# Running state by 64 tokens in place of 128, attention products on 64x64 quarters, every key turned by TensorE

## The chip, the cores and the metric

One Trainium2 chip; the kernel uses one of its cores. The metric is the device time of the launch in microseconds. Of the kernel before there are three timed runs and one profiled run.

## The reference

Decayed linear attention of four sequences of 768 tokens with eight heads of 64, and on its output a soft mixture of eight experts with four slots each. All data are float32.

```python
for b in range(nb):                                   # blocks of 64 tokens
    intra = np.einsum('bhic,bhjc->bhij', qb, kb) * Dmask[None]
    intra = np.einsum('bhij,bhjd->bhid', intra, vb)
    inter = np.einsum('bhid,bhde->bhie', qb * lam_pow[None], kv_state)
    out[:, :, sl] = intra + inter
    kv_state = lam_block * kv_state + np.einsum('bhsd,bhse->bhde', kb * rev_pow[None], vb)
...
logits = x @ phi                                      # x: 3072 x 512, phi: 512 x 32
d = softmax of logits over the tokens;  slot_input = d.T @ x
slot_out[e] = np.maximum(slot_input[e] @ w1[e], 0.0) @ w2[e]     # 8 experts, 512 -> 1024 -> 512
c = softmax of logits over the slots;   out = c @ slot_out
```

Dmask[i, j] is lam^(i-j) for i >= j and 0 above. The blocks are exact whatever their length, so a kernel may choose its own: it needs the masked product inside a block, the product of the decayed q with the state before the block, and the state's own step.

## The kernel before

The 3072 tokens are 24 chunks of 128 (T = 24, six to a sequence, NB = 6). The loop at line 442 takes one chunk a step. All engines run their instructions in the order in which the program writes them (the wrapper InOrder, whose line 51 all rows of the profile carry), so what stands in a step is set by that loop alone; nothing is reordered. A tile names a buffer; a pool gives a tile's tag so many buffers, and a writer waits until the readers of the buffer that it reuses are done.

A step does this. SP issues the loads of chunk t+2: q and k with the channels on the partitions, v with the tokens on them, and for nine of the chunks (loaded(), line 36) k a second time with the tokens on them, "kN". Between these it issues slabs of w1 (512 KB each), at a pace of PACE/10 a step up to NSLAB buffers; later loads of w2 ("w2t" of 256 KB into buffers that the attention leaves, "w2p" of 512 KB into slabs that the first expert product leaves) stand behind them. scores(t) multiplies k by q for pairs of 64 keys and 128 queries, on 64x64 quarters of the array, and DVE masks the two banks (at). recall(t) multiplies the state by the decayed q (qs, made by POOL) into the banks xa and xb. turn_k(t+1) transposes k on PE where it was not loaded, into the bank kv, and ACT copies it out (kn). natural(t-1) transposes a finished chunk (xt) back to tokens (x). attend(t) adds the masked products with v to xa and xb, 128 rows deep, and ACT copies them to xt. state(t) multiplies the decayed k (kd, POOL) by v into kv; DVE adds it to the decayed state (st), and POOL decays the sum for the next step (dec). Every fourth step has the logits of four chunks, the next one the transposes of their exponentials (weights), and the sums of the slots (slots) follow.

After the loop come the last chunk's part of the softmax, two first expert products (first, 64 matmuls each), two parts of the second (second), and the output, whose first tiles are written while the second part runs.

```python
442    for t in range(T):
463        scores(t)
467        recall(t)
471            turn_k(t + 1)
473                natural(t - 1)
488        attend(t)
501        decay_q(t + 1)
502        state(t)
503        decay_k(t + 1)
```

In the rows of the profile float32 matmuls have two records each, so that the 16 matmuls of scores are 32 records; transposes have one.

## Time and profile before

| | us |
|---|---|
| median of three runs | 169.73 (168.62 to 172.34) |
| the profiled execution | 170.31 |
| its span, from the first to the last instruction | 168.4 |
| PE busy in the span | 149.2 |
| DVE, POOL, ACT busy | 90.7, 64.4, 60.8 |
| DMA | 61.56 MB, mean 366 GB/s |

Times inside the profile count from the start of the span. "Busy" of PE is the union of its matmuls, weight loads are shown apart (PEld). The chain of waits follows the last instruction back to what released each piece of work. The page's groups give count, total busy time and the mean of one instruction in ns. Step 1 starts at 11.6 with its scores, step 22 at 106.3; the first expert product starts at 118.7.

### The profile page before, as it was taken

What the parts mean: (1) busy time and instruction counts of PE and PEld (TensorE: products, weight loads), DVE (VectorE), ACT (ScalarE), POOL (GpSimd) and SP (SyncE); (2) the same over time, 40 slices, a digit from 0 to 9 for tenths busy, and PEclk for the clock granted to TensorE, in tenths of its full rate; (3) what the DMA queues carried; (4) which work ended last, traced back from release to release, by engine and by line L of the source; (5) the groups of instructions that cost most, each with busy time, mean ns of one, the idle gap of its engine ahead of it and who ended that gap; (6) DMA issues with size and microseconds to landing.
All of it is one profiled execution on the core that took longest, in us unless ns stands there. A gap on an engine that the chain in (4) does not pass through costs nothing.

```text
span 168.4 us, 6282 instructions
## 1 busy us (share of the span) xinstructions
PE 149.2 (89%) x2629; PEld 108.0 (64%) x2629; DVE 90.7 (54%) x213; ACT 60.8 (36%) x153; POOL 64.4 (38%) x86
## 2 busy tenths in 40 slices
PE   6889998997979999979999799999899999999700
PEld 6668887686867889768868677776233345546600
DVE  2665453556475647565546537575118799245800
ACT  3033442443422444342344344225010698342700
POOL 1248772245665156655252556610000295000000
PEclk9999999999999999999999999999999999999965
DMA  5999999999999999999999999899999999999795
GB/s 170 350 330 308 373 399 409 410 407 407 416 405 405 374 402 404 408 415 405 407 409 386 387 329 337 261 289 273 390 399 408 411 399 408 403 375 314 262 384 195
DMA packets 32444, 61.56 MB, mean 366 GB/s; under 512 B 3616, under 2 KB 9760, under 8 KB 32416
## 3 DMA queue, kind: packets, MB, share of 16 engines
q1 hardware_dynamic: 32272, 61.16, 97.1%
q8 instruction: 21, 0.34, 0.8%
q14 instruction: 7, 0.06, 0.1%
q10 hardware_dynamic: 144, 0.01, 0.1%
HBM read 54.86 MB, written 6.29 MB: 363 GB/s over the span
## 4 chain that ended last, share of the span: by engine, by line
PE 65%; DMA 13%; DVE 10%; issue 4%; POOL 2%; ACT 1%; DVEq 0%; POOLq 0%; ACTq 0%; SPq 0%
PE xa L51 15%; PE kv L51 13%; PE sc L51 11%; PE gl L51 8%; PE xb L51 7%; PE tr L51 7%; PE dp L51 4%; DMA slab<-w_x 4%; DMA ld<-qT 4%; DMA ld<-kT 4%; DVE at L51 2%; DVE cs L51 2%; DVE CN L51 2%; DVE o L51 1%; DMA y<-o 1%
## 5 line engine op out<-in xcount | busy, mean ns | idle before, releaser
L51 DVE TENSOR_TENSOR at<-sc,mask 128x512 f32<-128x512 f32 x48 | 30.8, 683 | 9.9 <-PE sc L51 9.9
L51 PE MATMUL sc<-ld 64*64 64x128 f32 x768 | 27.8, 282 | 0.5 <-issue 0.5
L51 POOL TENSOR_TENSOR qs<-ld,qpow 128x512 f32<-128x512 f32 x20 | 25.7, 1285 | 5.9 <-DVE qpow L51 2.9
L51 PEld LDWEIGHTS sc<-ld 64*64 64x64 f32 x768 | 21.6, 136 | 6.4 <-issue 5.3
L51 ACT COPY x<-tr 128x512 f32<-128x512 f32 x24 | 14.1, 588 | 30.1 <-PE tr L51 30.1
L51 POOL TENSOR_TENSOR dec<-st,qpow 128x256 f32<-128x256 f32 x16 | 10.0, 622 | 28.1 <-DVE st L51 28.1
L51 PE MATMUL xa<-at,ld 128*64 128x128 f32 x192 | 15.8, 285 | 3.7 <-DVE at L51 3.7
L51 DVE TENSOR_TENSOR st<-dec,kv 128x256 f32<-128x256 f32 x16 | 6.8, 422 | 20.0 <-PE kv L51 20.0
L51 POOL TENSOR_TENSOR kd<-kn,mask 128x512 f32<-128x512 f32 x11 | 11.7, 1060 | 13.0 <-ACT kn L51 13.0
L51 PEld LDWEIGHTS xa<-at,ld 128*64 128x64 f32 x192 | 10.0, 136 | 8.3 <-DVE at L51 6.1
L51 ACT COPY kn<-kv 128x512 f32<-128x512 f32 x11 | 6.4, 586 | 23.9 <-PE kv L51 19.8
L51 PE MATMUL tr<-ident,xt 128*128 128x128 f32 x96 | 15.0, 279 | 0.0
L51 PE MATMUL xb<-at,ld 128*64 128x128 f32 x192 | 14.8, 275 | 0.0
L51 PE MATMUL kv<-ld,kd 128*64 128x64 f32 x320 | 12.8, 222 | 1.2 <-ACT kn L51 0.8
L51 PE MATMUL xa<-qs,st 64*64 64x128 f32 x160 | 12.3, 270 | 1.0 <-POOL dec L51 1.0
L51 PEld LDWEIGHTS kv<-ld,kd 128*64 128x64 f32 x320 | 12.1, 138 | 1.5 <-issue 1.5
L51 PE MATMUL xb<-qs,st 64*64 64x128 f32 x160 | 12.4, 270 | 0.0
L51 PEld LDWEIGHTS tr<-ident,xt 128*128 128x128 f32 x96 | 10.8, 142 | 2.4 <-issue 2.4
L51 POOL TENSOR_TENSOR kd<-ld,mask 128x512 f32<-128x512 f32 x9 | 9.5, 1060 | 5.1 <-DVE mask L51 5.0
L51 PEld LDWEIGHTS xb<-at,ld 128*64 128x64 f32 x192 | 10.8, 136 | 0.8 <-DVE at L51 0.7
L51 ACT COPY xt<-xa 128x256 f32<-128x256 f32 x24 | 8.8, 368 | 6.4 <-PE xa L51 6.3
L51 PEld LDWEIGHTS xa<-qs,st 64*64 64x64 f32 x160 | 9.5, 133 | 1.2 <-POOL dec L51 1.2
(134 smaller groups left out, 229.2 us busy)
## 6 DMA issues: line engine op xcount, KB each, us to landing
slab<-w_x SPq DMA_DIRECT2D x32, 512.0 KB, 6.9
w2p<-w_x SPq DMA_DIRECT2D x20, 512.0 KB, 9.4
ld<-qT SPq DMA_DIRECT2D x24, 256.0 KB, 6.2
ld<-kT SPq DMA_DIRECT2D x24, 256.0 KB, 5.8
ld<-vN SPq DMA_DIRECT2D x24, 256.0 KB, 6.9
w2t<-w_x SPq DMA_DIRECT2D x24, 256.0 KB, 5.4
y<-o SPq DMA_DIRECT2D x24, 256.0 KB, 3.5
ld<-kN SPq DMA_DIRECT2D x9, 256.0 KB, 5.6
```

The source lines that it names most:

```text
L51: return self._tc.keep_in_program_order(f(*args, **kwargs))
```

## The change

The state now goes forward by half a chunk, HF = 64 tokens. The masks and the powers are made for 64 positions, and every attention product works on a 64x64 quarter with 64 moving columns:

- scores: 16 matmuls as before, but each half of the keys meets its own half of the queries alone; DVE masks 256 columns a bank in place of 512.
- attend: each half of the tokens by itself. It comes in two calls. The first, "cross", takes for the rows of half j the heads of half 1-j; ACT reads two columns of its result (seen), and the second call, which does the other pairs, waits for that. gather() copies the finished banks to xt, as attend() did.
- recall: one product for each half of the chunk, with the state before that half. The first chunk of a sequence has one for its second half.
- state: 16 matmuls into two banks, ka and kb; DVE adds and decays twice (the decay was on POOL). The last chunk of a sequence, which had none, does the first half.
- k is turned on PE for all 24 chunks, two chunks ahead, with a bank of its own (tk); kN isn't loaded any more.
- scores(t+1) stand in step t, between the state's products and attend(t). Each step starts with state(t), and the logits run in one go with no step of the state between their parts.
- loads go as k four, v three and q four chunks ahead, ahead of the slabs; NLOAD 12 for 10, NSLAB 33 for 35, PACE 14 for 16.

TensorE's queue over a full step, before (here the step's scores are its last two rows, of 16 in all):

```order
L51 MATMUL kv<-ident,ld 128x128 x4
L51 MATMUL tr<-ident,xt 128x128 x4
L51 MATMUL xa<-at,ld 64x128 x4
L51 MATMUL xb<-at,ld 64x128 x4
L51 MATMUL kv<-ld,kd 64x64 x8
L51 MATMUL sc_726<-ld 64x128
L51 MATMUL sc_727<-ld 64x128
```

And TensorE's queue over the same work after the change, from the last rows of a step's scores to the first of the next step's state:

```order
L47 MATMUL sc_549<-ld 64x64
L47 MATMUL sc_550<-ld 64x64
L47 MATMUL xab<-at,ld 64x64 x8
L47 MATMUL tr<-ident,xt 128x128 x4
L47 MATMUL tk<-ident,ld 128x128 x4
L47 MATMUL xab<-at,ld 64x64 x8
L47 MATMUL xab<-qs,st 64x64 x16
L47 MATMUL ka<-ld,kd 64x64
L47 MATMUL kb<-ld,kd 64x64
```

The sizes are those of the result. The products of attend and of the state have twice the number at half the depth, the recall stands behind attend, and both transposes stand together between the two calls of attend.

DVE's queue over two steps without softmax work, before:

```order
L51 TENSOR_TENSOR at<-sc_726,mask 128x512
L51 TENSOR_TENSOR at<-sc_727,mask 128x512
L51 TENSOR_TENSOR st<-dec,kv 128x256
L51 TENSOR_TENSOR at<-sc_805,mask 128x512
L51 TENSOR_TENSOR at<-sc_806,mask 128x512
```

And after, one step and the start of the next:

```order
L47 TENSOR_TENSOR st<-dec,ka 128x256
L47 TENSOR_TENSOR dec<-st,qpow 128x256
L47 TENSOR_TENSOR at<-sc_1018,mask 128x256
L47 TENSOR_TENSOR at<-sc_1019,mask 128x256
L47 TENSOR_TENSOR st<-dec,kb 128x256
L47 TENSOR_TENSOR dec<-st,qpow 128x256
L47 TENSOR_TENSOR st<-dec,ka 128x256
```

Three instructions a step have become six, all of 256 columns, and the two decays came from POOL.

SP's queue from the last chunks' loads to the output, before:

```order
L51 DMA ld<-vN 128x512
L51 DMA ld<-kN 128x512
L51 DMA ld<-qT 128x512
L51 DMA ld<-kT 128x512
L51 DMA w2p<-w_x 128x2x512 x2
L51 DMA ld<-vN 128x512
L51 DMA w2t<-w_x 128x512 x24
L51 DMA w2p<-w_x 128x2x512 x17
L51 DMA y<-o 128x2x256 x24
```

And after:

```order
L47 DMA ld<-kT 128x512
L47 DMA ld<-vN 128x512
L47 DMA ld<-qT 128x512
L47 DMA slab<-w_x 128x1024 x2
L47 DMA ld<-vN 128x512
L47 DMA slab<-w_x 128x1024 x4
L47 DMA w2p<-w_x 128x2x512
L47 DMA w2t<-w_x 128x512 x24
L47 DMA w2p<-w_x 128x2x512 x19
L47 DMA y<-o 128x2x256 x24
```

Four slabs of w1 and a pair of w2 now stand behind the last load of the attention, where no slab stood, and 19 pairs behind the w2t in place of 17.

The diff, cut to what the steps below speak of (the line numbers of the kernel after are not those above):

```diff
+HF = P // 2
...
-NSLAB = 35
-NLOAD = 10
+NSLAB = 33
+NLOAD = 12
...
-PACE = 16
+PACE = 14
...
+    def load_step(s):
+        load("k", s + 2)
+        load("v", s + 1)
+        load("q", s + 2)
...
         for hp in range(HP):
             for j in range(2):
                 for hh in range(2):
                     r = slice(64 * hh, 64 * hh + 64)
+                    c = slice(hp * P + HF * j, hp * P + HF * j + HF)
                     pe.matmul(
-                        out=banks[hh][64 * j:64 * j + 64, hp * P:(hp + 1) * P],
-                        lhsT=k_[r, hp * P + 64 * j:hp * P + 64 * j + 64],
-                        rhs=q_[r, hp * P:(hp + 1) * P],
+                        out=banks[hh][HF * j:HF * j + HF, hp * HF:(hp + 1) * HF],
+                        lhsT=k_[r, c],
+                        rhs=q_[r, c],
                         start=True,
                         stop=True,
                     )
         AT[t] = []
         for hh in range(2):
-            at = work.tile([P, HP, P], F32, tag="at", name="at", bufs=2)
-            sc = banks[hh].rearrange("p (a b) -> p a b", a=HP)
+            at = work.tile([P, HP, HF], F32, tag="at", name="at", bufs=4)
+            sc = banks[hh][:, 0:HP * HF].rearrange("p (a b) -> p a b", a=HP)
             dve.tensor_tensor(out=at, in0=sc, in1=mask[:, hh], op=ALU.mult)
             AT[t].append(at)
     def decay_q(t):
...
+        if t >= T:
+            return
+        tk = bank("tk")
+        for hp in range(HP):
+            pe.transpose(tk[:, hp * P:(hp + 1) * P], IN["k", t][:, hp * P:(hp + 1) * P], ident)
+        KN[t] = tk
+    def keep_k(t):
+        if t >= T:
+            return
+        kn = work.tile([P, D], F32, tag="kn", name="kn")
+        act.copy(out=kn, in_=KN[t])
+        KN[t] = kn
+    def decay_k(t):
+        if t >= T:
+            return
+        kd = work.tile([P, H, DH], F32, tag="kd", name="kd")
+        pool.tensor_tensor(
+            out=kd.rearrange("p (a b) c -> p a b c", a=2),
+            in0=KN.pop(t).rearrange("p (b a c) -> p a b c", a=2, b=HP),
+            in1=kpow.rearrange("p (a b) o -> p a b o", a=2).broadcast_to([P, 2, HP, DH]),
+            op=ALU.mult,
+        )
...
+        KD[t] = kd
+    def state(t, j):
+        parts_ = 2 if t % NB < NB - 1 else 1
+        if j == 0:
+            v_ = IN["v", t].rearrange("p (h c) -> p h c", h=H)
+            kd = KD.pop(t)
+            KV[t] = [bank("ka"), bank("kb")][:parts_]
             for hp in range(HP):
+                for hh in range(2):
+                    for i, kv in enumerate(KV[t]):
+                        r = slice(HF * i, HF * i + HF)
+                        pe.matmul(
+                            out=kv[64 * hh:64 * hh + 64, hp * DH:(hp + 1) * DH],
+                            lhsT=kd[r, HP * hh + hp, :],
+                            rhs=v_[r, HP * hh + hp, :],
+                            start=True,
+                            stop=True,
+                        )
+            ST[t] = [ST["S"] if t % NB > 0 else None]
+        if j == parts_:
+            return
+        kvv = KV[t][j][:, 0:HP * DH].rearrange("p (a b) -> p a b", a=HP)
+        st = work.tile([P, HP, DH], F32, tag="st", name="st", bufs=4)
+        if t % NB == 0 and j == 0:
+            dve.tensor_copy(out=st, in_=kvv)
+        else:
+            dve.tensor_tensor(out=st, in0=ST["dec"], in1=kvv, op=ALU.add)
+        ST[t].append(st)
+        ST["S"] = st
+        if parts_ == 2:
+            dec = work.tile([P, HP, DH], F32, tag="dec", name="dec")
+            dve.tensor_tensor(out=dec, in0=st, in1=lamc.broadcast_to([P, HP, DH]), op=ALU.mult)
+            ST["dec"] = dec
...
         g, a = divmod(hp, 2)
+        return XB[t][hh][64 * a:64 * a + 64, g * P + HF * j:g * P + HF * j + HF]
+    def attend(t, cross):
+        if cross:
+            both = ps.tile([P, 2, 512], F32, tag="x", name="xab")
+            XB[t] = [both[:, hh] for hh in range(2)]
+        v_ = IN["v", t].rearrange("p (h c) -> p h c", h=H)
+        for hp in range(HP):
+            for j in range(2):
+                hh = 1 - j if cross else j
+                r = slice(HF * j, HF * j + HF)
+                pe.matmul(
+                    out=place(t, hh, hp, j),
+                    lhsT=v_[r, HP * hh + hp, :],
+                    rhs=AT[t][hh][r, hp, :],
+                    start=(cross and hp < 2),
+                    stop=True,
+                    skip_group_check=True,
+                )
+        if cross:
+            act.copy(out=seen, in_=both.rearrange("p a b -> p (a b)")[:, HF:513:512 - HF])
...
     def recall(t):
+        qs = QS.pop(t)
+        for j in range(2):
+            st = ST[t][j]
+            if st is None:
+                continue
             for hp in range(HP):
                 for hh in range(2):
                     r = slice(64 * hh, 64 * hh + 64)
                     pe.matmul(
+                        out=place(t, hh, hp, j),
                         lhsT=st[r, hp, :],
+                        rhs=qs[r, hp, j, :],
+                        start=False,
                         stop=True,
                         skip_group_check=True,
...
-        pl = bank("gl")
+        pl = bank("tk" if g == G - 1 else "sc0")
...
+    turn_k(0)
+    keep_k(0)
+    scores(0)
+    decay_k(0)
+    powers()
+    decay_q(0)
     for t in range(T):
...
+        last = t == T - 1
+        load_step(t + 2)
+        want = min(NSLAB, (t + 1) * PACE // 10 if t < T - 2 else NSLAB)
         load_early(want - sent)
         sent = max(sent, want)
...
-        for _ in range((2, 4, 3)[t - T + 3] if t >= T - 3 else 0):
+        for _ in range((8, 3)[t - T + 2] if t >= T - 2 else 0):
...
+        turn = t // 4 - 1 if t > 3 else None
+        if t == 0:
+            attend(0, True)
+            turn_k(1)
+            keep_k(1)
+        state(t, 0)
+        scores(t + 1)
+        state(t, 1)
+        decay_k(t + 1)
+        if t > 0:
+            attend(t, True)
+            natural(t - 1)
+        if last:
             load_one(work, "kd", 1)
             load_one(work, "kn", 1)
+            for _ in logits(G - 1):
+                pass
+        else:
+            turn_k(t + 2)
+            keep_k(t + 2)
+            if turn is not None and t % 4 == 0:
+                for _ in logits(turn):
+                    pass
+            if turn is not None and t % 4 == 1:
+                sm = slot_softmax(turn, weights())
+                next(sm)
+            if turn is not None and t % 4 == 2:
+                slots(turn)
+                for _ in sm:
+                    pass
+        attend(t, False)
+        recall(t)
+        gather(t)
+        if last:
+            break
+        decay_q(t + 1)
```

## The prediction

> **What bounds the kernel now.** I read the stages first, then the chain of waits, then the DMA part of the page. The first view gives the busy time of each engine in five stretches: the start, attention steps 1 to 21, the last two steps with the softmax that follows them, the expert products, and the writing out.

> ```profile
> core 0: us, PE busy (x) PEld busy (x) DVE busy (x) ACT busy (x) POOL busy (x), PEclk, DMA share, GB/s
> 0.00:11.60 11.60, 8.57 (x90) 7.37 (x90) 6.29 (x19) 2.82 (x5) 3.07 (x9) 1.00 0.82 293
> 11.60:106.30 94.70, 89.32 (x1920) 73.28 (x1920) 51.96 (x115) 34.62 (x92) 50.90 (x53) 1.00 1.02 389
> 106.30:118.70 12.40, 11.32 (x222) 8.78 (x220) 7.88 (x26) 4.31 (x13) 3.34 (x5) 1.00 0.89 269
> 118.70:151.50 32.80, 32.80 (x354) 13.30 (x354) 18.70 (x44) 14.65 (x35) 7.11 (x20) 1.00 1.05 400
> 151.50:168.40 16.90, 7.16 (x58) 5.32 (x58) 5.91 (x10) 4.37 (x9) 0.00 (x0) 0.78 0.83 289
> ```

> The second row is the stage that the change rewrites: 94.7 us for 21 steps. PE is busy for 89.3 us of it. The transfers move 389 GB/s, which is 94.7 x 0.389 = 36.8 MB; at the 400 GB/s of the fourth row that alone takes 92.1 us. So two resources are nearly full in this stage, and a gain on one is worth only the distance to the next.

> The chain of waits prices one whole step (start, us, what); the products between an earlier and a present state ("xa, xb" of a recall) fill 57.04 to 57.48.

> ```profile
> 55.54 0.46 PE kv L51 x16
> 56.00 1.03 PE sc L51 x32
> ...
> 57.48 0.59 PE kv L51 x4
> 58.06 0.44 PE tr L51 x4
> 58.50 0.59 PE xa L51 x8
> 59.09 0.44 PE xb L51 x8
> ...
> 61.58 1.01 PE gl L51 x32
> ...
> 65.55 0.37 PE dp L51 x2
> ...
> 67.85 0.99 PE gl L51 x8
> ```

> State 0.46, scores 1.03, recall 0.44, turning k 0.59, natural 0.44, attend 0.59 + 0.44: 3.99 us. The first piece after a change of tile shape is 0.15 dearer (0.59 against 0.44 for the same four transposes or eight matmuls), and that happens three times a step. Every four steps 1.01 + 0.37 + 0.99 come on top. For steps 1 to 21: 21 x 3.99, less 11 unturned k at 0.44, three missing states at 0.46 and three missing recalls at 0.44, plus five times 2.37, is 88.1 us, near the 89.3 of the row.

> **PE after the change.** What counts is how fast quarter products follow each other. The timeline of PE shows the recall, already on 64x64 quarters, with 128 moving columns.

> ```profile
> 56.86 0.27 PE L51 MATMUL xa<-qs,st 64*64 64x128 f32 x1
> 56.87 0.27 PE L51 MATMUL xb<-qs,st 64*64 64x128 f32 x1
> 56.87 0.27 PE L51 MATMUL xa<-qs,st 64*64 64x128 f32 x1
> 56.88 0.27 PE L51 MATMUL xb<-qs,st 64*64 64x128 f32 x1
> 56.97 0.27 PE L51 MATMUL xa<-qs,st 64*64 64x128 f32 x1
> ```

> Four start within 0.02 us and the next four 0.11 later: the quarters run side by side, and the columns set the pace. With 64 columns the state's row above has 16 records in eight pairs, 0.46 / 8 = 0.058 a pair. So I price a group of four with 64 columns at 0.058, 0.0145 a record. The lower bound is half of 0.11, 0.055; the upper is that the record rate seen here, 0.11 / 4 = 0.027, can't be beaten. I take 0.058, since the state's row has the same columns and the recall shows that four start nearly together.

> State, scores and recall become 32 records each, 8 x 0.058 = 0.47; attend splits into two times 16, 0.23 each; natural and turning stay at 0.44 each, and now every k is turned. Shapes change twice a step, not three times. Sum: 3 x 0.47 + 2 x 0.23 + 2 x 0.44 + 2 x 0.15 = 3.05. For 21 steps, less half a recall (0.23) in three, plus the same five times 2.37: 64.1 - 0.7 + 11.9 = 75.3, 12.8 less than 88.1.

> [...]

> **DVE and POOL.** The forms that change, from the page and the groups of instructions:

> ```profile
> L51 DVE TENSOR_TENSOR at<-sc,mask 128x512 f32<-128x512 f32 x48 | 30.8, 683 | 9.9 <-PE sc L51 9.9
> L51 POOL TENSOR_TENSOR dec<-st,qpow 128x256 f32<-128x256 f32 x16 | 10.0, 622 | 28.1 <-DVE st L51 28.1
> L51 DVE TENSOR_TENSOR st<-dec,kv 128x256 f32<-128x256 f32 x16 | 6.8, 422 | 20.0 <-PE kv L51 20.0
> L51 POOL TENSOR_TENSOR qs<-ld,qpow 128x512 f32<-128x512 f32 x20 | 25.7, 1285 | 5.9 <-DVE qpow L51 2.9 <-POOL kd L51 1.7 <-DMA ld<-qT 1.3
> L51 POOL TENSOR_TENSOR kd<-kn,mask 128x512 f32<-128x512 f32 x11 | 11.7, 1060 | 13.0 <-ACT kn L51 13.0
> ```

> In steps 1 to 21, 42 maskings shrink from 0.683 to 0.422 (the price of 256 columns in the state's row): -11.0. There are 39 state sums for 18: +8.9. 36 decays arrive from POOL, at 0.422 as well: +15.2. DVE goes from 52.0 to 65.1 before waits. POOL loses the decay and keeps 1.06 + 1.29 = 2.35 a step, under the 3.05 of PE.

> The new decay reads two tiles of SBUF. DVE's CN, of that form, shows what POOL does to it; the POOL rows are of the same moments.

> ```profile
> 38.25 0.89 DVE L51 TENSOR_TENSOR CN<-ce,cs 128x128 f32<-128x128 f32 x1
> ```
> ```profile
> 37.93 1.06 POOL L51 TENSOR_TENSOR kd<-kn,mask 128x512 f32<-128x512 f32 x1
> ```
> ```profile
> 57.19 0.29 DVE L51 TENSOR_TENSOR CN<-ce,cs 128x128 f32<-128x128 f32 x1
> ```
> ```profile
> 58.88 1.06 POOL L51 TENSOR_TENSOR kd<-kn,mask 128x512 f32<-128x512 f32 x1 [3.52 <-ACT kn L51]
> ```

> With POOL idle (3.52 us before 58.88) it takes 0.29; begun during a kd it takes 0.89 and ends just after it. So a decay costs between 0.42 and 0.42 + 1.29, a whole qs. Of the two in a step, the first falls on the qs that starts when the recall before has ended, some 0.4 left of it; the second falls behind the masks, when kd is about over. I take 0.4 for one in two, 18 x 0.4 = 7.2: DVE 72 us, below PE; all at 0.6 would make it 87. [...]

> **DMA.**

> ```profile
> HBM read 54.86 MB, written 6.29 MB: 363 GB/s over the span
> ...
> ld<-kN SPq DMA_DIRECT2D x9, 256.0 KB, 5.6
> ```

> A load of 256 KB is 0.262 MB. The nine natural k go: 2.36 MB, 5.9 us at 400 GB/s. Total traffic then needs (61.15 - 2.36) / 0.400 = 147 us. In steps 1 to 21 there are 63 loads and 29 slabs of 0.524 MB, 31.7 MB: 79 us. But PACE 14 and NSLAB 33 push weights behind step 21: then 2 slabs, 24 w2t, 20 w2p and the output remain, 1.05 + 6.29 + 10.49 + 6.29 = 24.1 MB. Before it was 12.4 x 0.269 + 32.8 x 0.400 + 16.9 x 0.289 = 21.3 MB in 62.1 us.

> **The sum.** Steps 1 to 21: DMA 79, PE 75.3, DVE 72. Before, the stage lay 2.6 above its highest bound (94.7 against 92.1). I add that, and 0.5 for each of five softmax steps: the logits now run in one go, their exponentials stand on ACT ahead of the copies out of xab, and the next step's first attend waits for those. Price, the ACT groups:

> ```profile
> L51 ACT ACTIVATE e<-gl,nm 128x128 f32<-128x128 f32 x5 | 1.8, 368 | 4.9 <-PE xa L51 4.9
> L51 ACT ACTIVATE alpha<-nm 128x1 f32<-128x1 f32 x5 | 1.4, 283 | 0.0
> ```

> 0.37 + 0.28 less what is free before the attend. That is 84.1; I round to 85 for three resources within 7 us of each other (bounds 79 and 94.7). The start stays at 11.6: a turning and two copies are added, half of the mask scans goes; bounds -1.5 and +1. After step 21, 24.1 MB at 400 GB/s is 60.3, plus what the last row loses by its 289 GB/s, 16.9 x (1 - 289/400) = 4.7: 65.0, if the hole in the third row (269 GB/s, 4.1 us) is filled by the two slabs, the w2p and the eight w2t that steps 20 to 22 now queue; 69 if not. PE's own tail is the old 62.1 and hides under it. Span 11.6 + 85 + 65 = 161.6. The profiled run took 170.31 for 168.4, 1.9 more: 163.5, against the median of 169.73 a gain of 3.7%. The new read of two columns ("seen") hides behind natural and turning, 0.88 us; uncovered it costs at most the 0.28 of alpha a step.

> **Rivals.**
> 1. DVE is the bound. For it: three kinds of its work grow, and the 0.89 of CN. At 0.6 on every decay plus 2.6 and 2.5 the stage takes 92, span 168.6, time 170.5; halfway 167. Against: idle POOL in the second half of a step. It decides from 0.5 on every decay.
> 2. Quarter records don't come faster than the 0.0275 that is the mean of the rows above. Place: the four quarter products, 128 records a step. A step costs 128 x 0.013 = 1.66 more, PE 75.3 + 35 = 110, stage 115, span 192, time 194: slower. It decides from about 0.019 a record: there 128 x 0.0045 x 21 = 12 us put PE at 87, and the stage, with 2.6 and 2.5, at 92, and the gain of 6.8 is gone. For it: no row shows a lower mean. Against: the spacing inside a group of four. [...]
> 3. The hole fills and the stage follows the DMA: the whole traffic 147 us, plus 2 at the start and 4.7 at the end: 154 to 157 with waits, time 156 to 159.
> A smaller one, more code to fetch, lies within the range:
> ```profile
> q8 instruction: 21, 0.34, 0.8%
> ```
> 1,200 more matmul records mean some nine packets more of 16 KB. What one costs PE no row shows; I take nothing, and the range's upper end has room for it.

> **Chances.** Forecast 0.52, its own range 159 to 168; rival 1 0.20; rival 2 0.15; rival 3 0.13. The range 156.5 to 173 leaves out most of rival 2 and a little of rival 1. About 2% is what a measurement tells from no change, 166.3 to 173.1. Faster: rival 3 and most of the forecast, 0.58. Same: the rest of it and most of rival 1, 0.23. Slower: rival 2 and the tail of rival 1, 0.19.

> **What would show it.** Right: scores of 32 records near 0.5 us, a step without softmax near 3.6 to 3.9, DVE's decay of 0.42 to 0.8, the stage to step 22 near 85, 0.40 TB/s from there to the last weights. Wrong: scores near 0.8 (rival 2); decays at 1 us and DVE back to back (rival 1); steps short but PE waiting for w2p in the second expert product, which would say that the weights were pushed too late and the 65 is the term that failed.

## The result, and the profile after

The changed kernel takes 200.47 us (median of four runs, 198.06 to 203.46), the kernel before 169.63 beside it: a ratio of 1.171, 95% interval 1.161 to 1.181. It is slower, by 31 us, where 6 us faster was forecast. Most kernels here have a slower state in some of their runs (202.59 and 203.46 beside 198.06 and 198.35 in this one), so differences are given between the lowest runs too: here 198.06 - 168.62 = 29 us. The profiled execution took 198.35 us with a span of 196.2.

The page of the changed kernel: the span, the busy times, PE's granted clock in tenths, the mean rate of the transfers, the queue of the instruction fetches, and the chain by engine.

```profile
span 196.2 us, 8808 instructions
...
PE 151.7 (77%) x3833; PEld 111.9 (57%) x3833; DVE 113.2 (58%) x278; ACT 71.4 (36%) x190; POOL 63.7 (32%) x78
...
PEclk9999995799987999999797999859999999999995
...
DMA packets 31157, 59.35 MB, mean 302 GB/s; under 512 B 3472, under 2 KB 9616, under 8 KB 31120
...
q8 instruction: 30, 0.49, 1.0%
...
PE 70%; issue 16%; DVE 9%; ACT 1%; DVEq 0%
```

No engine is full: PE fell from 89% of the span to 77, and the transfers from 366 to 302 GB/s. But "issue", time in which an engine waited for nothing that the profile shows, is 16% of the chain, where it was 4. The clock drops in several places.

The stages of the changed kernel (columns as in the prediction): attention steps 1 to 21 (step 22's first products start at 133.03, so the cut lies 1 us into it), and everything from the first expert product on.

```profile
11.60:134.00 122.40, 91.67 (x3024) 77.89 (x3025) 74.26 (x179) 44.30 (x126) 49.03 (x44) 0.90 0.83 287
```
```profile
146.30:196.20 49.90, 40.14 (x411) 18.66 (x411) 24.60 (x54) 19.05 (x43) 7.08 (x20) 0.95 1.01 362
```

From the first expert product it is 49.9 us, as before (118.7 to 168.4, 49.7). All of the loss lies ahead of that: 21 steps take 122 us, where 85 were forecast, and PE is busy in 92 of them.

What PE's time is made of shows in the chain of waits (start, us, what), at the largest "issue" rows:

```profile
22.00 2.53 issue
24.88 0.48 PE sc L47 x32
...
28.00 3.04 issue
...
53.32 3.21 issue
...
91.49 3.10 issue
...
124.01 2.64 issue
```

The products are quick: 0.48 for the 32 records of the scores. Between them PE stands still for up to 3.2 us. The timeline of PE shows where it stops, in the middle of a state's products, whose operands were there already:

```profile
27.73 0.23 PE L47 MATMUL kb<-ld,kd 64*64 64x64 f32 x2
27.78 0.22 PE L47 MATMUL ka<-ld,kd 64*64 64x64 f32 x1
31.04 0.26 PE L47 MATMUL kb<-ld,kd 64*64 64x64 f32 x1 [3.04 <-issue]
```

Next, the busy times in stretches that I cut at the ends of such stops. The counts in brackets behind PE and PEld are matmuls and weight loads:

```profile
18.80:24.53 5.73, 3.19 (x126) 2.87 (x127) 1.51 (x4) 1.88 (x5) 2.32 (x3) 1.00 0.98 335
24.53:31.03 6.50, 3.46 (x126) 3.00 (x126) 2.88 (x6) 1.88 (x5) 2.40 (x2) 0.95 0.93 337
...
50.00:56.50 6.50, 3.30 (x126) 2.80 (x126) 2.59 (x6) 1.98 (x5) 2.47 (x2) 1.00 0.91 332
56.50:61.00 4.50, 3.96 (x127) 3.57 (x127) 1.71 (x6) 1.29 (x5) 1.83 (x2) 0.63 0.57 194
```

Every stretch holds 252 to 254 records, whatever they are and however long it lasts; with PE's 105 semaphore and drain records, 3.5 a block on average, that is about 256. A packet of q8 is 16,384 bytes in the trace (0.49 MB / 30 on the page), which is 64 bytes for each of 256 instructions; and the 30 packets are one for every 256 of PE's 7,775 instructions (7,771 in the trace). So I read a stop as a wait for the next block of instructions. The DMA view around the stop of 28.00 agrees. From 24.6 to 28.6 us it has no packet of q8, from 28.6 to 29.7 it has this one, and from 29.7 to 31.0 none again:

```profile
q8 instruction: 1, 0.02, 5.8%
```

PE stops at 28.00; the packet comes 0.6 us later at the earliest, and PE goes on at 31.04, 1.3 us or more behind its end. So it is at every boundary: counted in steps of 256 rows of PE from 14.30 on, the first row behind each of the 24 boundaries up to 133 us starts 1.26 to 1.60 us after the end of a packet. The fetch is thus not hidden behind PE's work here: it sets the time of the stage.

### The profile page after: what moved, and what is told of

Its sections match the earlier page's. It is cut to its first block, busy times and chain, and to the rows that moved or that the text cites. A ratio compares the mean times of both kernels' runs of the same rounds, so it can differ in the third digit from the quotient of the medians.

```text
span 196.2 us, 8808 instructions
## 1 busy us (share of the span) xinstructions
PE 151.7 (77%) x3833; PEld 111.9 (57%) x3833; DVE 113.2 (58%) x278; ACT 71.4 (36%) x190; POOL 63.7 (32%) x78
## 3 DMA queue, kind: packets, MB, share of 16 engines
HBM read 52.50 MB, written 6.29 MB: 300 GB/s over the span
## 4 chain that ended last, share of the span: by engine, by line
PE 70%; issue 16%; DVE 9%; ACT 1%; DVEq 0%
PE xab L47 22%; PE sc L47 15%; PE ka L47 10%; PE tr L47 9%; PE tk L47 9%; PE kb L47 6%; DVE dec L47 2%; DVE at L47 2%; DVE st L47 1%; DVE o L47 1%; DVE acc L47 1%; DVE cs L47 1%; DVE CN L47 0%; DVE h L47 0%; ACT xt L47 0%
## 5 line engine op out<-in xcount | busy, mean ns | idle before, releaser
L47 POOL TENSOR_TENSOR qs<-ld,qpow 128x512 f32<-128x512 f32 (+1 forms) x24 | 28.4, 1182 | 66.4 <-issue 65.0
L47 PE MATMUL xab<-at,ld 64*64 64x64 f32 x768 | 25.0, 240 | 7.8 <-issue 6.6
L47 PEld LDWEIGHTS xab<-at,ld 64*64 64x64 f32 x768 | 18.5, 145 | 16.9 <-issue 14.5
L47 PE MATMUL sc<-ld 64*64 64x64 f32 x768 | 20.5, 236 | 8.6 <-issue 8.3
L47 DVE TENSOR_TENSOR dec<-st,qpow 128x256 f32<-128x256 f32 x40 | 24.9, 623 | 1.4
L47 PE MATMUL kb<-ld,kd 64*64 64x64 f32 x320 | 16.4, 241 | 7.9 <-issue 6.5
L47 PE MATMUL ka<-ld,kd 64*64 64x64 f32 x384 | 19.6, 236 | 3.7 <-issue 3.7
L47 DVE TENSOR_TENSOR at<-sc,mask 128x256 f32<-128x256 f32 x48 | 17.9, 414 | 7.2 <-PE sc L47 7.1
L47 PEld LDWEIGHTS ka<-ld,kd 64*64 64x64 f32 x384 | 16.4, 149 | 7.4 <-issue 7.4
L47 PE MATMUL xab<-qs,st 64*64 64x64 f32 x704 | 16.9, 231 | 0.2 <-issue 0.2
## 6 DMA issues: line engine op xcount, KB each, us to landing
ld<-kT SPq DMA_DIRECT2D x24, 256.0 KB, 5.6
ld<-qT SPq DMA_DIRECT2D x24, 256.0 KB, 4.2
ld<-vN SPq DMA_DIRECT2D x24, 256.0 KB, 4.5
w2t<-w_x SPq DMA_DIRECT2D x24, 256.0 KB, 5.0
y<-o SPq DMA_DIRECT2D x24, 256.0 KB, 3.4
```

What stands on the lines that cost most here:

```text
L47: return self._tc.keep_in_program_order(f(*args, **kwargs))
```

## The experiments

The theories: **F**, a block of 256 PE instructions takes some 5 us to come while the loads run, and the changed kernel's products use it up in less. **V**, the decay of the state on DVE, and its contention with POOL. **C**, the chain kn, kd, qs through ACT and POOL, with one buffer each.

**Fewer instructions, same columns.**

```diff
-        for j in range(2):
-            st = ST[t][j]
+        st = ST[t][0]
...
-                        rhs=qs[r, hp, j, :],
+                        rhs=qs[r, hp].rearrange("p j b -> p (j b)"),
```

> The changed kernel, but the recall multiplies all 128 queries of a chunk by the state at the chunk's start, in eight products of 128 columns in place of sixteen of 64. It leaves out the state at the middle of the chunk for the second 64 queries (that state is still made). TensorE's streamed columns are the same; about 160 products (some 640 to 770 of TensorE's 7,775 instructions, or three blocks of 256) are gone. Theory F (TensorE's instructions come in blocks of 256 and a block takes 5 to 6 us to arrive while the loads run): three blocks fewer, 12 to 18 us faster than the changed kernel, 182 to 189 us. Rivals V (VectorE with the decay of the state, or its shared access) and C (the chain of one-buffer tiles through ScalarE and GpSimd): nothing of theirs moves, 198 to 202 us.

Measured: 192.4 us (186.2 to 196.0), 8 us less than the changed kernel, 12 between the lowest runs (186.16 and 198.06), with 384 of PE's 3,833 matmul records gone. On F's side of the rivals' 198, and at the lower end of F's 12 to 18 or below it. The kernel leaves out a part of the recall, so its output is not the reference's.

**The kernel before, cut into small pieces.** This is the run that decides. Of the change it has the shorter products alone.

```diff
+            for i in range(2):
+                c = slice(hp * P + HF * i, hp * P + HF * i + HF)
...
-                        out=banks[hh][64 * j:64 * j + 64, hp * P:(hp + 1) * P],
-                        rhs=q_[r, hp * P:(hp + 1) * P],
+                            out=banks[hh][64 * j:64 * j + 64, c],
+                            rhs=q_[r, c],
...
-                        rhs=qs[r, hp, :],
+                        rhs=qs[r, hp, HF * i:HF * i + HF],
```

> The kernel before, complete, with each score product and each recall product of 128 columns issued as two of 64 columns: the same streamed columns, the same sums, the same work on every other engine, but 24 more products a chunk (TensorE's program grows from 5,358 to 7,534 instructions; the changed kernel has 7,775). At the changed kernel's rate for quarters of 64 columns (32 records in about 0.48 us) the 64 records of the scores take 0.96 us, where they took 1.03. Theory F: 8.5 blocks more at 5 to 6 us each against the 3.8 us a step of before, so it becomes about as slow as the changed kernel, 185 to 200 us, with stops of 1 to 3 us every 256 instructions. Rivals V and C, and any that lies in the changed kernel's decay, buffers or loads: no change, 168 to 172 us.

Measured: 199.3 us (194.5 to 201.1). With DVE, POOL, ACT, loads and buffers of the kernel before, it is about as slow as the changed kernel (200.5; between the lowest runs 194.5 against 198.1), so neither V nor C is needed to explain nearly all of the loss. Its page has 3,717 matmuls, and its stretches between two boundaries are again of 252 to 254 records:

```profile
PE 159.1 (83%) x3717; PEld 119.2 (62%) x3717; DVE 90.7 (47%) x213; ACT 61.2 (32%) x153; POOL 64.4 (33%) x86
```
```profile
28.27:33.80 5.53, 3.95 (x127) 3.50 (x126) 2.52 (x5) 1.33 (x3) 3.52 (x4) 1.00 0.93 313
33.80:38.54 4.74, 4.40 (x127) 3.76 (x127) 1.07 (x4) 1.59 (x5) 1.28 (x1) 1.00 0.97 322
```

The scores themselves are hardly slower in pieces: 64 records start within 0.98 us, against 0.92 for the 32 of the kernel before, and the recall's 32 within 0.63 against 0.55 for 16 (medians, first start to the next group's). That is 3 us in 24 steps, of the 30.

**The decay back on POOL.**

```diff
-            dve.tensor_tensor(out=dec, in0=st, in1=lamc.broadcast_to([P, HP, DH]), op=ALU.mult)
+            pool.tensor_tensor(out=dec, in0=st, in1=lamc.broadcast_to([P, HP, DH]), op=ALU.mult)
```

> The changed kernel, complete, with the decay of the state put back on GpSimd, where it was before; nothing else. Theory F: no change, 197 to 204 us. Rival V (VectorE's decay, 0.62 us on average, 40 times, and its contention with GpSimd hold up the chain): 5 to 15 us faster. Rival C (GpSimd's queue is the chain): 40 decays of about 1 us more on GpSimd, 5 to 20 us slower.

Measured: 202.5 us (195.2 to 206.5), no change that shows in this spread; the lowest run is 2.9 us below the changed kernel's lowest. V falls, which asked for 5 to 15 us less, and C as far as it lies in POOL's queue.

**Light loads**, in the changed kernel and later in the kernel before.

```diff
-        want = min(NSLAB, (t + 1) * PACE // 10 if t < T - 2 else NSLAB)
+        want = 0 if t < T - 2 else NSLAB
```

> The changed kernel, complete, with none of the 33 weight slabs loaded before step 22; all of them are asked for there. The whole is longer, since the transfers of the slabs now follow the attention (220 to 245 us); what counts is the time from 11.6 us to the end of step 21 and TensorE's stops in it, with only some 0.8 MB a step asked for. Theory F with a fetch that waits behind the loads: the stops go or shrink to under 0.5 us each and the stage goes from about 125 us to 85 to 95. Theory F with a fetch that is slow by itself: stops as before, stage 115 to 125. Rivals V and C: stage 115 to 125 with TensorE's waits on named tiles, not on nothing.

> The kernel before, complete, with none of its 35 weight slabs loaded before step 22, like the changed kernel with light loads, whose first expert product (the lookup of the last chunk's slots ahead of it) began 11.8 us earlier than with its own loads, at 134.0 in place of 145.9. What counts here is the same product, at 118.2 in the kernel before. If the loads hold up the kernel before through TensorE's fetch as they do the changed one, it comes 8 to 12 us earlier. If TensorE's columns set the stage and the fetch is just in time (a block resumes 1.25 to 2 us after its packet with a stop over 0.4 us only twice), it comes 0 to 5 us earlier, at 113 to 118, and stays 16 to 21 us ahead of the changed kernel with light loads: that part of the loss is then the fetch by itself, with no loads to wait behind.

Measured: 210.8 and 203.6 us in all. What counts is the stage. The busy times of 30 to 90 us, first of the changed kernel with its own loads, then with light ones, then of the kernel before with its own and with light loads:

```profile
30.00:90.00 60.00, 48.48 (x1623) 40.36 (x1622) 38.05 (x93) 23.03 (x66) 24.96 (x22) 0.91 0.78 272
```
```profile
30.00:90.00 60.00, 50.58 (x1824) 42.00 (x1825) 45.52 (x109) 26.86 (x78) 28.34 (x25) 1.00 0.58 167
```
```profile
30.00:90.00 60.00, 56.59 (x1178) 45.80 (x1179) 34.17 (x77) 22.86 (x61) 30.14 (x30) 1.00 1.04 405
```
```profile
30.00:90.00 60.00, 57.66 (x1236) 47.06 (x1232) 35.31 (x79) 23.20 (x63) 31.89 (x33) 1.00 0.66 202
```

At 126.5 pairs of records a block that is one block in 60 x 126.5 / 1623 = 4.7 us with the loads and 4.2 with light ones. The kernel before needs one in 6.4, and 6.1.

How much of the loss needs the weight loads shows where the same chunk is done. The copies that end the attention of chunk 20 (of 0 to 23), in the kernel before and the changed one with their own loads, then in both with light loads:

```profile
100.92 0.38 ACT L51 COPY xt<-xb 128x256 f32<-128x256 f32 x1
124.24 0.63 ACT L47 COPY xt<-xab 128x256 f32<-128x256 f32 x2
97.20 0.38 ACT L51 COPY xt<-xb 128x256 f32<-128x256 f32 x1
107.41 0.63 ACT L47 COPY xt<-xab 128x256 f32<-128x256 f32 x2
```

With its own loads the changed kernel is 124.87 - 101.30 = 23.6 us behind there, with light ones 108.04 - 97.58 = 10.5. So 13 of the 24 us need the weight loads, and 10 stay beside the attention's own loads. Soon after, from 99 to 100 us on, the light kernels ask for all the slabs that they left out, and the changed one's fetch gets slower than ever: 20 blocks from 13.72 to 98.85 take 4.3 us each, four from 103.38 to 129.24 take 6.5:

```profile
13.72:98.85 85.13, 70.36 (x2530) 58.60 (x2531) 60.91 (x143) 36.92 (x105) 39.51 (x36) 1.00 0.60 174
103.38:129.24 25.86, 17.99 (x507) 14.41 (x507) 13.79 (x37) 7.49 (x23) 7.79 (x8) 0.87 1.02 395
```

The first expert product comes after that, at 134.46 (146.30 with the own loads) and in the kernel before at 114.30 (118.66):

```profile
134.46 1.06 PE L47 MATMUL tk<-slab,e 128*32 128x512 f32 x8 [0.43 <-DVE wl L47]
```
```profile
114.30 1.06 PE L51 MATMUL gl<-slab,e 128*32 128x512 f32 x8 [0.44 <-DVE wl L51]
```

The kernel before came 4.4 us earlier and stayed 20.2 us ahead, as expected (0 to 5, and 16 to 21). But these 20 us are not the fetch with no loads to wait behind, as the expectation has it: half of them come after chunk 20, behind the slabs. Of the two forms of F with light loads neither came out: to step 22, at 116.40, the stage takes 105 us, between the 85 to 95 and the 115 to 125, and stops of up to 1.8 us stay between 30 and 90 us. The fetch is slow beside few loads (4.3 us a block beside 174 GB/s) and slower behind many (6.5 beside 395).

In the changed kernel with light loads PE still goes on 1.2 to 1.6 us after the end of a packet at 22 of 24 boundaries, with its own loads at all 24; in the kernel before at 7 of 16, with light loads at none, where the median is 3.5 us (worked out from the starts of the packets and of the records at the boundaries). The kernel before is thus just in time. What falls with lighter loads is mainly the time from the crossing of a boundary to the start of the next packet: a median of 1.7 us with light loads and of 2.7 with the own ones, and 3.8 to 4.2 in the four blocks behind the slabs. The packet itself takes a median of 1.0 to 1.1.

**How much an instruction costs.** Two runs cut only the recall's or only the scores' products; a third cuts the products of scores and values by output rows, so that none of the cut records has 64 columns.

```diff
-            for hp in range(HP):
+            for hp, c in [(hp, c) for hp in range(HP) for c in range(2)]:
                 pe.matmul(
-                    out=place(t, hh, hp),
-                    lhsT=v_[:, HP * hh + hp, :],
+                    out=place(t, hh, hp)[SL * c:SL * c + SL],
+                    lhsT=v_[:, HP * hh + hp, SL * c:SL * c + SL],
```

> The kernel before, complete, with only the recall's products cut into two of 64 columns each: 5,998 of TensorE's instructions in place of 5,358, or 2.5 blocks of 256 more. Theory F as a floor (a block takes about 5.2 us to come, as in the kernel with both products cut; the kernel before needs 6.4 us of work for one: 12 blocks in 76.4 us): some 20 blocks then lie in the same stage at 5.6 us each, still above the floor, so nearly nothing, 168 to 173 us. Theory F as a price for each instruction (30.2 us for the 2,176 instructions of both cuts): 8.9 us more, 176 to 180 us.

> The kernel before, complete, with only the scores' products cut into two of 64 columns each: 6,894 instructions, six blocks more. Floor: 23.5 blocks at 5.2 us in the stage are 122 us in place of 107, so 182 to 187 us. Price for each instruction: 21 us more, 188 to 193 us. If it is not the instructions but how quarters of 64 columns run: the scores are two thirds of the columns that were cut, 186 to 192 us here and 176 to 182 us with the recall alone cut, so the two runs together tell that from the floor.

> The kernel before, complete, with each of the eight products of scores and values a chunk cut by output rows into two of 32: 16 products of 128 columns, none of 64, and 768 more instructions (6,126). TensorE already runs such 128x32 products in the softmax's logits, 32 records in 1.01 us, against 0.93 us for the 16 records here: 1.9 us in 24 steps by the columns alone. If instructions cost (12 to 14 ns each, as in the kernels with the recall or the scores cut): 9 to 11 us more, 177 to 182 us. If records of 64 columns cost, and not the count: 169 to 172 us.

And one goes the other way, with the scores as eight products of 64x128:

> The kernel before, complete, with the scores as eight products of 64x128 on halves of the array in place of sixteen of 64x64 on quarters, each of 128 columns: the same streamed time if two halves run side by side, and 768 instructions fewer (4,590). Floor: the kernel before is at most at the edge of it, so 166 to 170 us. Price for each instruction: 768 of 2,176 of 30.2 us, 10.7 us faster, 156 to 160 us.

All four are the complete kernel before, with the same sums; the rows on the kernel before, on the changed one and on both cuts stand beside them (the packets are those of q8; each ratio is to runs of the kernel before on the same chip):

| kernel | PE matmul records | packets | us, median (range) | against before |
|---|---|---|---|---|
| scores 64x128 | 2,245 | 18 | 170.95 (170.65 to 171.58) | 1.013 (1.009 to 1.018) |
| before | 2,629 | 21 | 169.07 (167.75 to 170.14) | |
| recall cut | 2,949 | 23 | 177.88 (174.47 to 181.26) | 1.040 (1.028 to 1.052) |
| attend cut | 3,013 | 24 | 177.95 (175.55 to 179.34) | 1.041 (1.036 to 1.047) |
| scores cut | 3,397 | 27 | 187.10 (184.87 to 189.38) | |
| scores and recall cut | 3,717 | 29 | 199.27 (194.53 to 201.14) | |
| the changed kernel | 3,833 | 30 | 200.47 (198.06 to 203.46) | 1.171 (1.161 to 1.181) |

By the medians it is nearly a line from before upward: (199.27 - 169.07) / (3,717 - 2,629) = 0.028 us a record, 14 ns for each of its two instructions. The changed kernel lies near it, 1,204 records and 30.8 us above before. Between the lowest runs (of the kernel before on the same chip) it bends: 6.0 us for the recall's 320 records, 6.8 for the attend's 384, 16.4 for the scores' 768, 26.8 for both cuts' 1,088, 29.4 for the change's 1,204, so 0.018 to 0.025 us a record, more for the later ones. It is a price near this kernel, not a constant.

The attend's cut, with records of 128 columns, costs 8.5 us, as the recall's with 64 does (9.0). PE's own time explains at most 1.9 of that, by the expectation's count; the rest goes by the count of instructions and not by the shape. The "floor" that I had expected to spare the recall's cut (168 to 173 us) fails: a block of dense products is late even where the average block is not. In that run PE goes on 1.2 to 1.6 us behind a packet at 11 of the 16 boundaries up to 112 us, against 7 of 16 in the kernel before. Downward nothing comes back. 384 records fewer are 1.9 us slower; there the scores take 1.09 us a step in place of 0.92 (24 x 0.17 = 4 us). In that kernel no boundary waits any more: PE reaches each of the 13 up to 112 us at least 2.2 us after its packet. Since its scores are dearer, it does not tell what the seven late boundaries of the kernel before cost.

**The gains of the change without its instructions.** Only the zero quarter of the scores is left out; in one of two runs all keys but the first chunk's are turned, too. Both also start with three warming products in place of nine, two of which clear the banks of the scores.

```diff
+                    c = slice(hp * P + 64 * j, (hp + 1) * P)
                     pe.matmul(
-                        out=banks[hh][64 * j:64 * j + 64, hp * P:(hp + 1) * P],
+                        out=banks[hh][64 * j:64 * j + 64, c],
...
-    return t == 0 or t % NB in (2, 4)
+    return t == 0
```

> The kernel before, complete, with two things that add hardly an instruction (5,391): the later 64 keys of a chunk are multiplied by the later 64 queries alone (the other quarter of the scores is zero after the mask; the banks are cleared once at the start), and the keys of all chunks but the first are turned on TensorE, so that eight transfers of 0.26 MB go. It takes the changed kernel's two gains, fewer columns (a quarter of the scores' 1.03 us a step, about 0.26 us) and fewer loads, without its instructions. Floor: TensorE does a step in about 0.2 us less with the eight turns counted, 163 to 168 us. If TensorE's columns do not set the stage at all: 167 to 171 us.

> The kernel before, complete, with only the zero quarter of the scores left out (the later 64 keys by the later 64 queries alone); the keys are loaded and turned as before, 5,331 instructions. The scores' group took 0.77 us in the kernel that had this and the turned keys, 0.92 us in the kernel before. Where TensorE's columns set the step: 24 times 0.15 us, 165 to 167 us. Where a step is set by the fetch or the loads: no change, 168 to 170 us.

Measured: 168.72 us, a ratio of 0.996 (0.992 to 1.001), and 169.54, 1.000 (0.996 to 1.003). The scores do take 0.77 us in place of 0.92, and nothing comes of it; with the turned keys (0.49 us a chunk more on PE, 2.1 MB less to load) hardly anything either. My reading, which no run shows, is that PE, the loads and the fetch are so near to each other in the kernel before that one or two of them eased are not enough. None of these kernels is faster than the kernel before.

## Why the prediction was wrong

- **PE's rate.** Right. A group of four at 0.058, 0.0145 a record, gave 0.47 for the scores. The timeline of the changed kernel has 32 records in 51.50 - 51.01 = 0.49:

```profile
51.01 0.68 PE L47 MATMUL sc<-ld 64*64 64x64 f32 x32
51.50 0.46 PE L47 MATMUL xab<-at,ld 64*64 64x64 f32 x16
```

  Rival 2 said that records don't come faster than 0.0275 on the mean; that mechanism falls, at 0.49 / 32, 0.015 a record over the quarters, though its time (194) was the nearest of all.
- **The step that failed** is the one on code: "What one costs PE no row shows; I take nothing, and the range's upper end has room for it." The nine packets came (21 to 30 on q8). A packet is not a cost of 1 us beside PE's work but a gate for it: beside these loads a block each 4.7 us on average (single ones 3.6 to 6.5), however little time its products need. My step of 3.05 us holds 128 quarter records and 8 transposes, 136 pairs, 1.07 blocks: the fetch needs 5.0 us for it. 21 steps and five times the softmax's 42 records, 3,066 in all, are 24.2 blocks, 114 us, where the sum had 85; 122 were measured, as the blocks outside of 30 to 90 us were slower still. The profile of before did bear a sign. A product that waits for nothing stops there too, inside the scores:

```profile
28.31 0.55 PE L51 MATMUL sc<-ld 64*64 64x128 f32 x12 [0.46 <-issue]
```

- **DVE.** The mask and the state's sum came as priced (0.414 and 0.417 on average for 0.422). The decay is 0.62 on average, between my 0.42 and 0.42 + 1.29, and it bounds nothing: 74 us of 122. Rival 1 falls, as the decay on POOL shows.

```profile
L47 DVE TENSOR_TENSOR dec<-st,qpow 128x256 f32<-128x256 f32 x40 | 24.9, 623 | 1.4
```

- **DMA and the end.** From 134.0 it took 196.2 - 134.0 = 62.2 us, 65 forecast, but not shown to be for the reason given: the transfers move 205 GB/s from 132 to 145 us and 362 after 146.30, not the 0.40 TB/s that was to be the sign, and PE's own tail, 62.1 before, gives the same time. The traffic fell by the 2.36 MB of kN, which gained nothing that shows: the queues are not full in the stage (287 GB/s, DMA share 0.83; 389 and 1.02 before), which I put down to the steps that ask for loads coming late. Rival 3 falls.
- **The signs to look for.** Scores near 0.5 and decays of 0.42 to 0.8 on average were named as right, and both were seen. A step near 3.6 to 3.9 and the stage near 85 were named too, and both were missed: 122 / 21 is 5.8 us a step, those with softmax work included. No sign for wrong named what went wrong, PE waiting for nothing.

## What to carry to other kernels

Count TensorE's instructions as a resource like its columns: here a float32 matmul was two matmul and two weight-load records (768 and 768 for the 384 of the scores), and in the changed kernel 256 instructions took 4.3 us on average to come beside 174 GB/s of loads, 4.7 beside 272, and 6.5 beside 395. Halving the columns at twice the number of matmuls gained nothing here: with scores and recall cut the kernel before went from 169.1 to 199.3 us. It had little room for that: between 30 and 90 us it needed a block in 6.4 us, and at 7 of 16 boundaries PE already went on 1.2 to 1.6 us behind a packet. To see how near a kernel is, divide its stage into blocks of 126 matmul records, as they came here, and look for "issue" stops in the middle of a group whose operands are ready.

## What the runs showed of the hardware that I had not expected

```profile
31.03:36.30 5.27, 5.26 (x101) 4.71 (x104) 2.88 (x6) 1.33 (x3) 1.06 (x1) 0.50 0.70 257
```
```profile
126.65:132.00 5.35, 5.35 (x111) 4.90 (x114) 3.42 (x9) 1.33 (x3) 1.06 (x1) 0.50 0.98 362
```

  In the traces of both kernels all records of the clock but the last are 3.41 us long or a multiple of that. Here are two stretches of 3.41 us, each with the next one; PE is idle for 2.0 us in the first and for 1.8 in the third:

```profile
102.03:105.44 3.41, 1.38 (x41) 1.17 (x33) 1.34 (x4) 0.16 (x1) 1.35 (x2) 1.00 0.72 265
105.44:108.86 3.42, 3.42 (x94) 3.09 (x96) 0.78 (x3) 2.12 (x5) 0.61 (x1) 0.50 0.79 273
64.48:67.89 3.41, 1.57 (x48) 1.51 (x47) 1.99 (x5) 0.38 (x2) 1.99 (x2) 1.00 0.98 345
67.89:71.30 3.41, 2.75 (x86) 1.60 (x85) 2.58 (x5) 1.63 (x4) 1.13 (x1) 1.00 0.73 247
```

  So it is in the profiles of all 13 kernels (worked out from the records of the clock and of PE): from 8 to 160 us the clock fell to 0.50 after 24 such stretches (5 of them in the changed kernel, with 1.91 to 2.80 us idle), in 23 of which PE and its weight loads were idle for 1.87 us or more (in one for 1.72), and it stayed at 1.00 after all with 1.83 or less but that one. The stage's mean clock is 0.90 (1.00 before). How much of the 31 us that adds to the stops wasn't measured by itself. With light loads the window of 30 to 90 us has a clock of 1.00, and a block still takes 4.2 us there: the fetch holds the steps up without it.
